# Attention and token-mixing kernel: scores on 64-key halves shifted by 64 queries, value products on row halves in two parts, reciprocal as an operation of its own, a new order

## The chip, the cores and the metric

The kernel runs on one core of one Trainium2 chip. The metric is device time in microseconds (us); the kernel before takes 134.45 us (median of 3 runs, 134.01 to 134.52). TensorE is called PE, its weight loads PEld, VectorE DVE, ScalarE ACT, GpSimd POOL and SyncE SP, as in the profile.

## The reference

The inputs `q`, `k`, `v` have 8 batches, 8 heads, 576 positions and 64 features. A query sees its own key and the 127 before it, with a bias per head that falls with the distance. The attention output, heads side by side, is `x` (8 x 576 x 512), which goes through a token mixer.

```python
scores = scale * np.matmul(q, k.transpose(0, 1, 3, 2))
mask = (rel >= 0) & (rel < window)          # window = 128, rel = query - key
scores = np.where(mask, scores + bias[None], -1000000000.0)
attn = softmax(scores)                      # exp, divided by its sum
attn_out = np.matmul(attn, v)
...
wq = x @ w_q ; wk = x @ w_k                 # 512 -> 64
W_tok = scale * np.einsum('bsd,btd->bst', wq, wk)
mixed = np.einsum('bst,btd->bsd', W_tok, x)
return np.maximum(mixed, 0.0) @ w_out
```

## The kernel before, in words

**Staging.** For each batch `b` the rows of q and k come in as float16 tiles `nat` of 128 positions (operations `Lq`, `Lk`: one DMA for each of four tiles `n`), v as tiles `vt` (`Lv`, with a column of ones beside the 64 values). The last 64 positions of two neighbouring batches come together (`Lt`, `Lv..4`: tiles `natt`, `vtl`). `TQ` and `TT` transpose q and k on PE with an identity, 64 rows of the array at a time, and `ETQ`/`ETT` copy the result to `qkT`.

**Attention.** `QK b,g,u` computes scores of key block `g` (128 keys) for four heads `u`: four products of 64 features by 128 keys by 256 queries, on the upper and lower row half of the array by turns (block 3 has 192 queries and then 64 keys of the tail, so eight products). `EXP` on ACT takes the 1024 columns of a unit to the tile `pt`; `MUL` on DVE multiplies the 2048 columns of both units by `bias`, which also holds the mask. `PV b,t` multiplies `pt` (128 keys by 128 queries as weights) with `vt` (65 columns): 8 heads by 2 key blocks are 16 products, 8 for t = 0, and 32 on column halves for the two tails (t = 4). `X` on DVE takes the reciprocal of the ones column and then multiplies.

**Mixer.** `XT` transposes `x`, `EXT` copies it to `xT`; `WQ`, `WK`, `G` and `MX` are the products of the mixer, `RM` its relu, `OUT` the last product, `EO` copies its result to `osb`, and `DO` writes it to memory, from POOL for batches 0 to 5 and from SP for 6 and 7.

**Order.** Nothing is scheduled at run time. The text `ORDER` lists every operation with its engine and, for PE, its PSUM bank pair (`@PE:2`, or `@PE:01` for one bank; `+3` puts three idle-time products `fill` ahead of it). Each engine runs its own operations in the order of that list. There are 4 bank pairs, 6 tiles `pt`, 4 sets of `nat` and of `vt`. The loads are DMAs that POOL issues one after another; the loop `for d in late: d.deps += issues` makes every output of batches 0 to 5 wait until all loads are issued. `apart` and `lone` (called for every operation) tell the framework which dependences between banks and columns it may drop.

`mode` is the tiling of the array that an operation uses: 0 all of it, 1 row halves (64 x 128), 2 column halves (128 x 64), 3 quarters (64 x 64).

Of the kernel before, what the change touches and what calls it, by code (L numbers as in the profile page):

```python
# [14 lines left out]
P = 128  # L15
# [12 lines left out]
NPT = 6  # L28
HELD = 26
# [12 lines left out]
EXP0.1.0@ACT ones1@DVE QK0.1.1@PE:1+2/30 ETQ0.1.1.1@DVE QK0.0.1@PE:3 Lq1.1@POOL EXP0.1.1@ACT
QK0.2.1@PE:0+1 TT0@PE:2 Lq1.0@POOL EXP0.2.1@ACT ETT0@DVE ETT1@DVE QK0.3.1@PE:1+1 Lv0.0@POOL
MUL0.1@DVE QK0.3.0@PE:2 EXP0.0.1@ACT Lv0.1@POOL EXP0.3.0@ACT MUL0.2@DVE TQ1.2@PE:0+5 Lw0@POOL
Lv0.2@POOL ETQ1.2@ACT MUL0.0@DVE Lv0.3@POOL EXP0.3.1@ACT QK1.3.1@PE:0+6/30 QK1.3.0@PE:2 QK1.2.0@PE:3
Lk2.0@POOL EXP1.3.1@ACT TQ1.0@PE:1 MUL0.3@DVE Lv0.4@POOL ETQ1.0@ACT PV0.0@PE:0 Lq2.0@POOL X0.0@DVE
EXP1.3.0@ACT PV0.1@PE:1 wqq@DVE Lv1.3@POOL QK1.1.1@PE:0 MUL1.3@DVE QK1.1.0@PE:2 EXP1.1.1@ACT
Lq2.1@POOL EXP1.1.0@ACT X0.1@DVE PV0.2@PE:0 Lv1.2@POOL X0.2@DVE EXP1.2.0@ACT Lw1@POOL QK1.0.0@PE:1
QK1.2.1@PE:2 Lk2.1@POOL MUL1.1@DVE EXP1.2.1@ACT PV0.3@PE:0 Lv1.1@POOL XT0.0@PE:3 EXP1.0.0@ACT
MUL1.2@DVE QK1.0.1@PE:2 Lv1.0@POOL EXT0.0@ACT PV0.4@PE:1 X0.3@DVE Lk2.3@POOL EXP1.0.1@ACT  # L50
WQ0.0@PE:30 X0.4@DVE Lq2.2@POOL XT0.1@PE:0 PV1.3@PE:2 EXT0.1@ACT MUL1.0@DVE Lk2.2@POOL XT0.2@PE:31
XT1.2@PE:10 TQ2.0@PE:0 EXT0.2@ACT EXT1.2@ACT Lq2.3@POOL WK0@PE:31 EWQ0.0@DVE ETQ2.0@ACT X1.3@DVE
PV1.2@PE:1 Lk3.2@POOL WQ0.1@PE:30 EWK0@ACT X1.2@DVE PV1.0@PE:0 Lwo0@POOL EWQ0.1@ACT QK2.0.1@PE:2
X1.0@DVE Lwo3@POOL PV1.1@PE:1 EXP2.0.1@ACT Lwo2@POOL QK2.0.0@PE:3 X1.1@DVE G0@PE:00 EXP2.0.0@ACT
Lwo1@POOL XT1.1@PE:2 EG0@DVE Lt2.1@POOL XT1.0@PE:1 EXT1.1@ACT MUL2.0@DVE MX0.0@PE:0 MX0.1@PE:3
EXT1.0@ACT Lv2.0@POOL TQ2.2@PE:2 RM0.0@ACT WQ1.0@PE:10 ETQ2.2@DVE Lt2.0@POOL WQ1.1@PE:11 RM0.1@ACT
WK1@PE:00 Lq3.0@POOL EWQ1.1@DVE QK2.2.0@PE:2 EWQ1.0@DVE EWK1@ACT QK2.2.1@PE:3 Lq3.3@POOL
EXP2.2.0@ACT MX0.4@PE:1 G1@PE:00 RM0.4@DVE Lk3.3@POOL OUT0.3@PE:01 EXP2.2.1@ACT EG1@DVE Lq3.2@POOL
MX1.4@PE:1 QK2.1.1@PE:2 EO0.3@DVE MX1.1@PE:3 RM1.4@ACT EXP2.1.1@ACT Lk3.0@POOL OUT0.1@PE:00
RM1.1@DVE Lq3.1@POOL TT2@PE:1 EO0.1@ACT QK2.1.0@PE:2 MUL2.2@DVE MX1.0@PE:3 EXP2.1.0@ACT Lk3.1@POOL  # L60
OUT1.4@PE:01 ETT2@DVE RM1.0@ACT Lk4.1@POOL OUT0.0@PE:00 ETT3@DVE MUL2.1@DVE Lv2.1@POOL QK2.3.1@PE:2
EO0.0@ACT QK2.3.0@PE:1 TQ3.2@PE:3 EXP2.3.1@ACT EO1.4@DVE Lv2.4@POOL OUT1.1@PE:00 ETQ3.2@DVE
EXP2.3.0@ACT Lv2.3@POOL PV2.0@PE:2 OUT1.2@PE:01 X2.0@DVE Lv3.3@POOL EO1.1@ACT QK3.3.1@PE:3 EO1.2@ACT
MUL2.3@DVE Lv2.2@POOL TQ3.0@PE:1 EXP3.3.1@ACT QK3.3.0@PE:2 OUT1.3@PE:00 Lq4.0@POOL ETQ3.0@DVE
EXP3.3.0@ACT PV2.1@PE:3 Lk4.0@POOL EO1.3@ACT QK3.1.1@PE:1 X2.1@DVE QK3.1.0@PE:2 Lq4.1@POOL
EXP3.1.1@ACT OUT0.2@PE:01 MUL3.3@DVE Lv3.1@POOL EXP3.1.0@ACT XT2.0@PE:3 QK3.0.1@PE:1 Lq4.2@POOL
EXT2.0@DVE OUT1.0@PE:00 EXP3.0.1@ACT MUL3.1@DVE Lk4.3@POOL PV2.2@PE:2 EO0.2@ACT QK3.2.0@PE:3
Lq4.3@POOL EO1.0@ACT X2.2@DVE PV2.3@PE:1 EXP3.2.0@ACT QK3.2.1@PE:0 Lv3.2@POOL X2.3@DVE PV2.4@PE:2
EXP3.2.1@ACT TQ4.0@PE:3 Lk4.2@POOL X2.4@DVE XT2.1@PE:1 ETQ4.0@ACT WQ2.0@PE:00 Lk5.2@POOL EXT2.1@DVE
XT2.2@PE:01 QK3.0.0@PE:2 EWQ2.0@DVE XT3.2@PE:10 Lv3.0@POOL EXT2.2@ACT QK4.0.0@PE:3 MUL3.2@DVE  # L70
EXP3.0.0@ACT WK2@PE:11 Lt4.1@POOL WQ2.1@PE:00 EXP4.0.0@ACT EWK2@DVE QK4.0.1@PE:2 MUL3.0@DVE
Lk5.3@POOL G2@PE:01 EWQ2.1@ACT EXP4.0.1@ACT Lq5.3@POOL PV3.2@PE:3 EG2@DVE MX2.1@PE:0 X3.2@DVE
EXT3.2@ACT Lq5.2@POOL MX2.0@PE:2 RM2.1@ACT TQ4.2@PE:1 RM2.0@DVE Lq6.3@POOL PV3.3@PE:3 ETQ4.2@ACT
OUT2.3@PE:00 Lt4.0@POOL X3.3@DVE PV3.0@PE:2 EO2.3@ACT QK4.2.0@PE:1 Lv4.1@POOL X3.0@DVE PV3.1@PE:3
EXP4.2.0@ACT Lv4.0@POOL QK4.2.1@PE:0 X3.1@DVE OUT2.0@PE:20 EXP4.2.1@ACT Lq5.1@POOL MUL4.0@DVE
XT3.0@PE:1 EO2.0@ACT QK4.1.1@PE:3 Lk5.1@POOL XT3.1@PE:0 EXT3.0@ACT OUT2.2@PE:21 EXT3.1@DVE
EXP4.1.1@ACT Lq5.0@POOL MUL4.2@DVE QK4.1.0@PE:1 TT4@PE:0 EO2.2@ACT Lk5.0@POOL TQ5.2@PE:3
EXP4.1.0@ACT ETT4@DVE WQ3.1@PE:20 ETQ5.2@DVE Lv4.2@POOL WK3@PE:21 ETT5@ACT EWQ3.1@ACT Lk6.1@POOL
QK4.3.1@PE:1 MUL4.1@DVE EWK3@ACT QK4.3.0@PE:0 MX2.4@PE:3 EXP4.3.1@ACT G3@PE:20 Lv4.3@POOL RM2.4@DVE
WQ3.0@PE:21 EXP4.3.0@ACT Lq6.0@POOL EG3@DVE PV4.0@PE:1 EWQ3.0@DVE MX3.1@PE:3 X4.0@DVE PV4.1@PE:2  # L80
Lq6.2@POOL RM3.1@ACT MX3.0@PE:0 X4.1@DVE TQ5.0@PE:1 Lq6.1@POOL RM3.0@ACT QK5.3.1@PE:3 ETQ5.0@DVE
OUT2.1@PE:20 Lv4.4@POOL EXP5.3.1@ACT Lv5.3@POOL QK5.3.0@PE:0 EO2.1@DVE XT4.0@PE:1 EXP5.3.0@ACT
QK5.0.0@PE:3 EXT4.0@DVE OUT3.1@PE:21 Lk6.0@POOL MUL4.3@DVE EXP5.0.0@ACT Lk6.2@POOL QK5.2.0@PE:1
QK5.0.1@PE:0 WQ4.0@PE:20 EO3.1@ACT MUL5.3@DVE Lk6.3@POOL PV4.2@PE:3 EXP5.0.1@ACT OUT3.3@PE:21
Lv5.0@POOL X4.2@DVE EXP5.2.0@ACT PV4.3@PE:0 Lv5.1@POOL MUL5.0@DVE QK5.1.1@PE:3 EWQ4.0@ACT MX3.4@PE:1
EO3.3@ACT Lk7.3@POOL OUT3.2@PE:20 EXP5.1.1@ACT RM3.4@DVE X4.3@DVE Lk7.2@POOL PV4.4@PE:1 EO3.2@ACT
QK5.2.1@PE:3 X4.4@DVE Lt6.1@POOL TQ6.0@PE:0 EXP5.2.1@ACT TQ6.2@PE:2 ETQ6.0@DVE Lt6.0@POOL
OUT3.0@PE:10 ETQ6.2@ACT Lq7.2@POOL MUL5.2@DVE QK5.1.0@PE:3 EO3.0@ACT XT4.2@PE:11 Lv5.2@POOL
XT4.1@PE:0 QK6.1.1@PE:2 EXP5.1.0@ACT EXT4.1@DVE OUT3.4@PE:10 Lq7.3@POOL EXT4.2@DVE EXP6.1.1@ACT
MUL5.1@DVE WK4@PE:11 Lq7.0@POOL PV5.0@PE:0 EO3.4@ACT QK6.1.0@PE:3 X5.0@DVE Lk7.1@POOL EWK4@ACT  # L90
# [76 lines left out]
def kernel(  # L167
# [51 lines left out]
    def two(bank):  # L219
        return pairs[bank[0]]  # L220

    held = []

    def hold(i):
        held.append(i.ins)

    def mm(*a, **k):
        hold(nc.tensor.matmul(*a, **k))  # L228

    def tp(*a):  # L230
        hold(nc.tensor.transpose(*a))  # L231

# [658 lines left out]
```

## Time and profile before

| | |
|---|---|
| median of 3 runs | 134.45 us (134.01 to 134.52) |
| profiled execution, span of its instructions | 132.4 us |
| PE | 121.7 us busy, 2349 products |
| ACT | 112.9 us busy |
| DVE | 112.3 us busy |
| POOL | 109.6 us busy (almost all DMA issue) |
| PE from 28.00 to 127.40 us | 98.80 us busy of 99.40 |

The profile is one execution. Its span runs from the first to the last instruction and is 2.05 us shorter than the median of the runs, which also hold what lies around the span. An operation's length on PE is read here from its first product's start to the next operation's first start, since matmuls are pipelined and the shown ends overlap. The names of the program stand for lines: all products are on L228, transposes on L231, loads on L383, outputs on L797 and L800, `EXP` on L556, `MUL` on L566, reciprocal and multiplication on L613 and L614.

### The profile page before, as it was taken

The page shows a single profiled execution, that of the slowest core. Times are in us where ns is not written, and L with a number is a line of the kernel's source. Part 1 is how long each engine was busy: PE and PEld are TensorE (multiplying, and loading weights), DVE is VectorE, ACT ScalarE, POOL GpSimd, SP SyncE. Part 2 cuts the span into 40 slices and gives each one's busy share as a digit, 9 for nine tenths or more (in the row PEclk, how much of TensorE's full clock was granted, in tenths as well). Part 3 has the DMA queues.
Part 4 walks back from the last instruction along what each step waited for, and adds up shares of the span by engine and source line. Part 5 has one row for each costly group of instructions (what it writes and reads, how often), then busy time and mean ns, then how long its engine had stood idle before and what let it go on. Part 6 is the DMA issues. An engine that isn't in the chain of part 4 may idle for free.

```text
span 132.4 us, 5423 instructions
## 1 busy us (share of the span) xinstructions
PE 121.7 (92%) x2349; PEld 77.6 (59%) x2349; DVE 112.3 (85%) x206; ACT 112.9 (85%) x163; POOL 109.6 (83%) x147
## 2 busy tenths in 40 slices
PE   6988795888999999999999999999999999999970
PEld 2343364676774565767677667567567656863430
DVE  6776958997978999999999999999999999982530
ACT  5999779986999999999999999999999897554730
POOL 7999879999999999999999999999968509790000
PEclk9999999999999999999999999999999999999998
DMA  3999999999999999999999999999999936999775
GB/s 119 275 148 155 157 158 152 149 151 149 189 156 158 156 155 153 157 153 154 156 154 156 153 152 153 156 157 152 157 212 376 374 125 228 334 303 367 285 211 185
DMA packets 110663, 25.12 MB, mean 190 GB/s; under 512 B 104816, under 2 KB 107888, under 8 KB 110640
## 3 DMA queue, kind: packets, MB, share of 16 engines
q0 software_dynamic: 108128, 21.37, 178.4%
q1 hardware_dynamic: 2512, 3.41, 7.5%
q8 instruction: 18, 0.29, 0.8%
q14 instruction: 5, 0.04, 0.1%
HBM read 29.62 MB, written 9.44 MB: 295 GB/s over the span
## 4 chain that ended last, share of the span: by engine, by line
PE 77%; ACT 7%; POOL 6%; DMA 6%; issue 1%; POOLq 0%; ACTq 0%
PE pair L228 67%; PE pair L231 10%; DMA nat<-in_q_dram 6%; ACT pt L556 5%; POOL nat L383 4%; ACT qkT L241 1%; POOL natt L383 1%; ACT osb L235 1%; POOL ident masks.py:199 0%; POOL ident masks.py:197 0%; POOL xT L339 0%; POOL xT L340 0%; POOL wint L311 0%; ACTq L556 0%; POOLq L311 0%
## 5 line engine op out<-in xcount | busy, mean ns | idle before, releaser
L556 ACT ACTIVATE pt<-pair 128x1024 f16<-128x1024 f32 x64 | 63.2, 1033 | 1.6 <-PE pair L228 1.3
L383 POOL DMA_DIRECT2D vt<-in_v_dram x32 | 31.7, 1138 | 0.9 <-DMA nat<-in_q_dram 0.9
L228 PE MATMUL pair<-wout_sb,rm 128*128 128x512 f16 (+1 forms) x132 | 32.4, 374 | 0.0
L383 POOL DMA_DIRECT2D nat<-in_k_dram x29 | 29.2, 1059 | 0.5 <-DVE pt L566 0.5
L383 POOL DMA_DIRECT2D nat<-in_q_dram x29 | 29.0, 1058 | 0.1
L566 DVE TENSOR_TENSOR pt<-pt,bias 128x2048 f16<-128x2048 f16 x24 | 29.0, 1217 | 0.0
L228 PE MATMUL pair<-vt,pt 128*128 128x65 f16 (+1 forms) x512 | 21.4, 194 | 2.9 <-ACT pt L556 1.6
L228 PE MATMUL pair<-qkT 64*128 64x256 f16 (+2 forms) x320 | 23.3, 250 | 0.8 <-DVE qkT L243 0.3
L228 PEld LDWEIGHTS <-pt 128*128 128x128 f16 (+1 forms) x576 | 19.0, 100 | 8.1 <-issue 6.0
L614 DVE TENSOR_TENSOR x<-pair,inv 128x512 f16<-128x512 f32 x32 | 22.1, 692 | 1.1
L235 ACT COPY osb<-pair 128x512 f32<-128x512 f32 (+1 forms) x29 | 16.7, 585 | 4.3 <-PE pair L228 4.0
L797 POOL DMA_DIRECT2D out_dram<-osb x24 | 13.5, 604 | 6.4 <-ACT osb L235 4.7
L228 PEld LDWEIGHTS <-rm 128*128 128x128 f16 x132 | 10.9, 97 | 11.9 <-issue 1.9
L228 PEld LDWEIGHTS <-qkT 64*128 64x128 f16 x320 | 10.8, 94 | 8.3 <-issue 4.7
L731 ACT ACTIVATE rm<-pair 128x1024 f16<-128x1024 f32 (+1 forms) x12 | 11.3, 956 | 1.4 <-PE pair L228 1.2
L228 PE MATMUL pair<-fill 128*128 128x512 f16 x33 | 10.6, 453 | 1.7 <-DVE fill L364 1.2
L243 DVE COPY qkT<-pair 128x2048 f16<-128x2048 f16 (+1 forms) x12 | 10.4, 884 | 1.5 <-PE pair L231 1.5
L231 PEld LDWEIGHTS <-nat 64*128 64x128 f16 x512 | 9.1, 95 | 4.0 <-ACT nat L235 1.3
L231 PE MATMUL pair<-identh,nat 64*128 64x64 f16 x512 | 10.4, 190 | 1.1 <-DMA nat<-in_q_dram 0.7
L566 DVE TENSOR_TENSOR pt<-pt,biasl 128x2048 f16<-128x2048 f16 x8 | 9.7, 1219 | 1.6 <-ACT pt L556 1.6
L228 PE MATMUL pair<-xT,wqq_sb 128*128 128x256 f16 (+1 forms) x64 | 10.4, 287 | 0.0
L241 ACT COPY qkT<-pair 128x1024 f32<-128x1024 f32 (+1 forms) x10 | 8.2, 834 | 1.5 <-PE pair L231 1.4
(66 smaller groups left out, 161.8 us busy)
## 6 DMA issues: line engine op xcount, KB each, us to landing
out_dram<-osb POOLq DMA_DIRECT2D x24, 256.0 KB, 4.7
vt<-in_v_dram POOLq DMA_DIRECT2D x32, 128.0 KB, 6.0
nat<-in_q_dram POOLq DMA_DIRECT2D x28, 128.0 KB, 5.7
nat<-in_k_dram POOLq DMA_DIRECT2D x28, 128.0 KB, 5.8
out_dram<-osb SPq DMA_DIRECT2D x7, 256.0 KB, 2.6
out_dram<-osb POOLq DMA_DIRECT2D x6, 128.0 KB, 4.3
nat<-in_k_dram SPq DMA_DIRECT2D x1, 512.0 KB, 3.8
nat<-in_q_dram SPq DMA_DIRECT2D x1, 512.0 KB, 4.7
```

The lines of the kernel that those rows point to most:

```text
L228: hold(nc.tensor.matmul(*a, **k))
L231: hold(nc.tensor.transpose(*a))
L235: hold(nc.scalar.copy(out_ap, in_ap))
L241: hold(nc.scalar.copy(out_ap.bitcast(FP32), in_ap.bitcast(FP32)))
L243: hold(nc.vector.tensor_copy(out=out_ap, in_=in_ap))
L383: op = add(kind, b, part, (eng,), deps, lambda o: q.dma_start(out=dst, in_=src), size=size)
L556: nc.scalar.activation(out=pt[:, u, 0:1024], in_=two(s.bank).rearrange("p e c -> p (e c)"), func=AF.Exp, scale=SCALE)
L566: nc.vector.tensor_tensor(out=pt[:, :, 0:1024], in0=pt[:, :, 0:1024], in1=bt, op=ALU.mult)
L614: nc.vector.tensor_tensor(out=x.rearrange("p (g h d) -> p g h d", g=2, h=4), in0=pxv[:, :, :, 0:64], in1=inv.unsqueeze(3).broadcast_to([P, ...
L731: hold(nc.scalar.activation(out=out_ap, in_=in_ap, func=AF.Relu, scale=WSCALE))
L797: q.dma_start(out=out[b, P * st:P * st + P, c], in_=osb)
```

## The change

**Scores.** A unit now has two halves of 64 keys. The lower half takes 192 queries from its own first key on, the upper half (keys 64 to 127) takes 192 queries that start 64 later. Both have the same 192 columns of distances, so `bias`, `EXP` and `MUL` are 192 columns wide where they were 256: 768 columns for `EXP`, 1536 for `MUL`. Each unit is eight products of 64 x 64 (twelve for block 3) on quarters of the array.

**Value products.** In `pt` a head now has a slot of 256 columns, 192 of data and 64 of zeros in front of it (`gaps`, six operations at the start). Each half of 64 keys is read with its own shift, the zeros standing for queries outside. So a `PV` becomes products of 64 rows on the row halves of the array. The two row halves may not add to the same bank at once; so `PV` does heads 0 to 3 on one row half and 4 to 7 on the other, and a second part `PW` does the same with the row halves exchanged. Between the two, SP carries a mark: `T` is an empty instruction on SP that waits for `PV`, and `PW` waits for it.

**The rest.** `R` (reciprocal) and `X` (multiplication) are two operations. The zeroing of `qkT` and of half of `vtl` and the 16 small ones-writes are gone; one write of ones and the six `gaps` take their place. The rule that outputs wait for all load issues is gone. `ORDER` is new throughout.

```diff
-zeros@DVE iota@POOL Lf1.0@SP pads@POOL dist@DVE mask@DVE Lf0.0@SP ident@POOL ones2@DVE bias0@ACT
+iota@POOL Lf0.0@SP ones@DVE gaps0@ACT gaps3@ACT ident@POOL Lf1.0@SP dist@DVE mask@DVE Lh1.1@POOL
...
-    pt_s = [cpool.tile([P, 2, 1024], F16, name=f"pt{i}") for i in range(NPT)]
+    pt_s = [cpool.tile([P, 9 * HW], F16, name=f"pt{i}") for i in range(NPT)]
...
+    def behind(i, op):
+
+        for j in op.insts[-2:]:
+            tc.add_manual_dep(i, j.name, mybir.DependencyInfo(
+                mybir.DependencyClass.Sync, mybir.DependencyReason.DATA), reason="other half, same bank")
...
+    def mk_gaps(i):
         def em(o):
-            for t in vt_s[i]:
-                nc.vector.memset(t[:, :, D:D + 1], 1.0)
...
+            cpw(o.eng, pt_s[i].rearrange("p (s c) -> p s c", c=HW)[:, :, 0:64],
+                zero.rearrange("p (s c) -> p s c", c=64))
...
-    def segs(g):
-        return [(g, P * g, 256, 0)] if g < 3 else [(3, 384, 192, 0), (4, 512, 64, 192)]
+    def segs(g, c):
+
+        k0 = P * g + 64 * c
+        if g == 3 and c:
+            return [(k0, k0, 128, 0), (512, 512, 64, 128)]
+        return [(k0, k0, KW, 0)]
+
+    def data(t, lo, n):
+
+        return t[:, 64:64 + 8 * HW].rearrange("p (s c) -> p s c", c=HW)[:, lo:lo + n, 0:KW]
...
-                for kb, q0, wd, c0 in segs(g):
-                    for e in range(2):
-                        r = slice(64 * e, 64 * e + 64)
-                        mm(ps[:, e, 256 * a + c0:256 * a + c0 + wd],
-                                         t[r, 1, hp, P * kb:P * kb + P],
-                                         t[r, 0, hp, q0:q0 + wd], start=True, stop=True)
+                for e, c in ((0, 0), (1, 1), (0, 1), (1, 0)):
+                    r = slice(64 * e, 64 * e + 64)
+                    for k0, q0, n, at in segs(g, c):
+                        mm(ps[64 * c:64 * c + 64, e, KW * a + at:KW * a + at + n],
+                           t[r, 1, hp, k0:k0 + 64], t[r, 0, hp, q0:q0 + n], start=True, stop=True)
...
-            nc.vector.tensor_tensor(out=pt[:, :, 0:1024], in0=pt[:, :, 0:1024], in1=bt, op=ALU.mult)
+            nc.vector.tensor_tensor(out=data(pt, 0, 8), in0=data(pt, 0, 8), in1=bt, op=ALU.mult)
...
+        def em(swap):
+            def go(o):
+                px = two(o.bank or o.same.bank)
+                kbs = [(qt, 0)] + ([(qt - 1, 128)] if qt else [])
+                for i in range(4):
+                    for n, (kb, c) in enumerate(kbs):
+                        for u in range(2):
+                            r = u ^ swap
+                            h, at, cols = spot(i, u)
+                            at += c + 64 * (1 - r)
+                            k = slice(64 * r, 64 * r + 64)
+                            mm(px[:, u, cols], pt_s[turn(b, kb) % NPT][k, at:at + P],
+                               vt_s[b % NV][kb][k, h, 0:65], start=(swap + i + n == 0),
+                               stop=(swap == 1 and i == 3 and n == len(kbs) - 1))
+                if swap:
+                    behind(held[0], o.deps[0])
+
+            return go
...
+        p = add("PV", b, qt, PE, need, em(0), banks=2, mode=mode, size=size)
+
+        def mark(o):
+            hold(nc.sync.nop())
+            behind(held[0], p)
+
+        t = add("T", b, qt, SP, [p], mark)
+        w = add("PW", b, qt, PE, [t, p], em(1), mode=mode, size=size)
...
-    for d in late:
-        d.deps += issues
```

The first place is on PE: a score unit of block 3 followed by a value product, before (a unit of block 2 there) and now. The columns are line, instruction, output and inputs; 64 x or 128 x is the output's partitions and columns.

```order
L228 LDWEIGHTS qkT0_87
L228 MATMUL pair1_136<-qkT0_87 128x256
L228 LDWEIGHTS pt1_108
L228 MATMUL pair3_138<-vt30_101,pt1_108 128x65 [waits DVE_49]
L228 LDWEIGHTS pt2_109
L228 MATMUL pair3_138<-vt31_102,pt2_109 128x65
```

```order
L240 LDWEIGHTS qkT1_88
L240 MATMUL pair2_121<-qkT1_88 64x128
L240 LDWEIGHTS qkT1_88
L240 MATMUL pair2_121<-qkT1_88 64x64
L240 LDWEIGHTS qkT1_88
L240 MATMUL pair2_121<-qkT1_88 64x192
L240 LDWEIGHTS pt4_95 [waits SP_sequencer_49]
L240 MATMUL pair1_120<-vt_89,pt4_95 128x65
```

The score products are narrower and more, and the first weight load of a second part `PW` waits for SP where a value product waited for DVE alone.

The second place is on POOL: the end of the loads. Before, the last k load of batch 7 (`nat_84`), then v loads (`vt`), and outputs (`osb`) only behind the last of them; each waits for one of the eight semaphores `DMASW0` to `DMASW7`, that is for the landing of the DMA eight issues earlier.

```order
L383 DMA nat_83<-in_q_dram 128x8x64 [waits DMASW2_49]
L383 DMA nat_84<-in_k_dram 128x8x64 [waits DMASW3_49]
L383 DMA vt_97<-in_v_dram 128x8x64 [waits DMASW4_49]
L383 DMA vt_102<-in_v_dram 128x8x64 [waits DMASW5_49,PE_49]
L383 DMA vt_104<-in_v_dram 128x8x64 [waits DMASW6_49]
```

```order
L394 DMA nat30_83<-in_q_dram 128x8x64 [waits DMASW1_49]
L394 DMA natt1_86<-in_q_dram 64x16x64 [waits DMASW2_49]
L394 DMA vt_89<-in_v_dram 128x8x64 [waits DMASW3_49]
L856 DMA out_0_dram<-osb512_1291 128x512 [waits DMASW4_49,DVE_49]
L394 DMA vt_89<-in_v_dram 128x8x64 [waits DMASW5_49]
L856 DMA out_0_dram<-osb512_1531 128x512 [waits DMASW6_49,DVE_49]
L394 DMA vt_89<-in_v_dram 128x8x64 [waits DMASW7_49,PE_49]
L856 DMA out_0_dram<-osb512_1189 128x512 [waits DMASW0_49]
```

Behind the last q load of batch 7, outputs now stand between the v loads of batches 6 and 7; they come from batches 0 to 5, finished long before.

More of the change, by code (lines that the diff above doesn't have):

```diff
@@ L42 @@
[L42 to L47, printed above, removed]
@@ L119 @@
+EO7.3.1@ACT OUT7.1@PE:30 RM7.0@DVE DO7.3.0@SP DO7.3.1@SP OUT6.0@PE:31 EO7.1@DVE OUT6.1@PE:20 EO6.0@ACT
+DO6.0@SP OUT7.2@PE:21 EO6.1@ACT DO7.1@SP RM7.4@ACT OUT7.0@PE:20 EO7.2@ACT DO6.1@SP DO7.2@SP OUT7.4@PE:21
+EO7.0@DVE DO7.0@SP EO7.4@ACT DO7.4@SP
 """
```

317 lines of the change are left out of this document (167 added, 150 removed).

## The prediction

> **What bounds the kernel now.** I read the page's busy times, then the chain that ended last, then busy time in four stretches, to see which engine sets the end and where.
>
> ```profile
> span 132.4 us, 5423 instructions
> PE 121.7 (92%) x2349; PEld 77.6 (59%) x2349; DVE 112.3 (85%) x206; ACT 112.9 (85%) x163; POOL 109.6 (83%) x147
> PE 77%; ACT 7%; POOL 6%; DMA 6%; issue 1%; POOLq 0%; ACTq 0%
> ...
> 9.14 7.34 DMA nat<-in_q_dram
> 22.11 4.70 ACT pt L556 x5
> 115.84 11.51 PE pair L228 x102
> ...
> 0.00:17.00 17.00, 13.66 (x179) 6.32 (x179) 13.08 (x43) 14.17 (x23) 15.40 (x26) 1.00 1.64 170
> 17.00:28.00 11.00, 8.40 (x199) 6.12 (x190) 8.98 (x16) 10.57 (x12) 10.47 (x13) 1.00 2.27 152
> 28.00:127.40 99.40, 98.80 (x1980) 64.67 (x1980) 90.19 (x149) 86.95 (x127) 83.69 (x110) 1.00 1.92 195
> 127.40:132.40 5.00, 0.81 (x8) 0.48 (x5) 0.00 (x0) 1.21 (x3) 0.00 (x0) 0.92 0.65 227
> ```
>
> The last four rows give the stretch, its length, then the busy time of PE, PEld, DVE, ACT, POOL, the granted clock, DMA share and GB/s. Until 17 us the kernel waits for loads; from 17 to 28 us ACT is the busiest (10.57 of 11.00: the scores' exponentials); from 28 us to the chain's last product at 115.84 + 11.51 = 127.35 us PE is busy for 98.80 of 99.40 us at full clock; 5.0 us of copies and outputs end the span. So nothing that DVE or ACT save after 28 us is worth anything by itself. What PE saves counts, unless PE then has to wait. What could it wait for? POOL, that issues the loads:
>
> ```profile
> 84.81 1.33 POOL L383 DMA_DIRECT2D nat<-in_k_dram  x1
> 85.67 1.28 POOL L383 DMA_DIRECT2D vtl<-in_v_dram  x1
> 86.48 1.34 POOL L383 DMA_DIRECT2D nat<-in_q_dram  x1
> 87.35 1.35 POOL L383 DMA_DIRECT2D nat<-in_k_dram  x1
> 88.22 7.48 POOL L383 DMA_DIRECT2D vt<-in_v_dram  x8
> 95.15 2.20 POOL L797 DMA_DIRECT2D out_dram<-osb  x3
> 98.02 0.55 POOL L797 DMA_DIRECT2D out_dram<-osb  x1 [0.67 <-DMA vt<-in_v_dram]
> ...
> nat<-in_k_dram POOLq DMA_DIRECT2D x28, 128.0 KB, 5.8
> vt<-in_v_dram POOLq DMA_DIRECT2D x32, 128.0 KB, 6.0
> ...
> 97.23 0.64 PE L231 MATMUL pair<-identh,nat 64*128 64x64 f16 x32
> ```
>
> A load occupies POOL for 0.87 us (eight v loads start over 95.15 - 88.22 = 6.93 us), whatever PE does, and lands 5.8 to 6.0 us after its issue. The k load at 87.35 us is the last q or k load of the program; it lands at 93.2 us and its transposes start at 97.23 us. That is a slack of only 4 us, at a place from which PE still runs 127.35 - 97.23 = 30.1 us. The load stream is thus a second bound close under the first.
>
> **The price of PE work.** The timeline of PE gives an operation's length as the distance of starts.
>
> ```profile
> 42.59 1.04 PE L228 MATMUL pair<-wout_sb,rmt 128*128 128x512 f16 x4
> 43.47 1.03 PE L228 MATMUL pair<-wout_sb,rm 128*128 128x512 f16 x4
> 44.43 0.62 PE L228 MATMUL pair<-qkT 64*128 64x192 f16 x16
> ...
> 86.51 0.39 PE L228 MATMUL pair<-qkT 64*128 64x256 f16 x4
> 86.83 0.66 PE L228 MATMUL pair<-vt,pt 128*128 128x65 f16 x16
> 87.43 0.39 PE L228 MATMUL pair<-qkT 64*128 64x256 f16 x4
> 87.75 0.63 PE L228 MATMUL pair<-x,wkn 128*64 128x256 f16 x8
> 88.21 0.28 PE L228 MATMUL pair<-xtl,wkn 128*64 128x256 f16 x2
> 88.42 0.41 PE L231 MATMUL pair<-identh,natt 64*128 64x64 f16 x16
> 88.66 0.38 PE L228 MATMUL pair<-qkT 64*128 64x256 f16 x4
> ...
> 112.83 1.13 PE L228 MATMUL pair<-vt,pt 128*128 128x65 f16 x32
> 113.80 0.60 PE L228 MATMUL pair<-xT,wqq_sb 128*128 128x256 f16 x4
> ...
> 26.85:27.47 0.62, 0.62 (x32) 1.00 2.31 144
> ```
>
> Two value products on the whole array take 113.80 - 112.83 = 0.97, so 0.485 each, when the next operation uses the array in the same way; 0.60 (86.83 to 87.43) when it goes on to row halves. The last product takes 0.88 (42.59 to 43.47) and then 0.96 (to 44.43) in the same comparison. A change of tiling thus costs about 0.10 us. A score unit, 0.32 with a change behind it, is 0.22: two pairs of 256 columns.
>
> *Scores.* Eight products of 192 columns. If four run at once, a unit is two rounds of 192 columns at the rate of the pairs, 0.22 x 192/256 = 0.167 us. If only two run at once, it is four rounds, 0.33. Both sides have rows: sixteen transposes on row halves take 0.24 (88.42 to 88.66), and ten products of 256 columns on column halves 0.67 - 0.10 (87.75 to 88.42), 0.114 a pair, so both ways of halving overlap fully; the two together no row shows. Weights must come in fast enough too: the 32 tail products, a 64-column load each, took 0.62 - 0.10 (the last row, from their first start to the next operation's), 0.016 a load; eight would take 0.13, less than 0.167. I take 0.167: 64 units save 64 x 0.055 = 3.5 us.
>
> The Trainium skill (TensorEngine Tiling (Array Packing), Restrictions) says that column tiling disables fast weight load, and its page TensorE: Matmul & The Clock Gate (LDWEIGHTS) gives columns / 1.2 ns for a load, 53 ns for 64 columns. Eight such loads in a row would make a unit 0.43 us, an estimate from that page; the 0.016 us a load of the row above speaks against it.
>
> *Value products.* Sixteen products on the whole array become twice sixteen on row halves, that run in pairs; the sixteen transposes of 0.24 are the same shape, 64 columns for 65. So 2 x 0.24 = 0.48 for 0.485. The bound above is a part that pays as much as one on the whole array, 0.97. Taken: nothing. The parts now share their tiling with the transposes, but the scores no longer do: counted along the order of PE, changes of tiling go from 115 to 122 (without `fill`), +0.7 us.
>
> *The wait of the second part.* A `PW` can start when `PV` has drained, SP has seen it and PE has seen SP. Nearest rows:
>
> ```profile
> 110.10 0.42 PE L228 MATMUL pair<-vt,pt 128*128 128x65 f16 x8
> ...
> 110.63 0.21 DVE L613 RECIPROCAL inv<-pair 128x8 f32<-128x8 f32 x1 [0.17 <-PE pair L228]
> ```
>
> The products of 110.10 end at 110.52 and DVE starts 0.11 later. From the start of the last product: 0.19 of drain, 0.11 to SP, as much back, 0.4 us. PE is in order, so the whole rest of its queue stands behind a waiting `PW`. In the new order every `PV` behind the first two batches but four has 0.33 us or more of other work in front of its `PW` (a score unit and two changes of tiling, say, 0.37). With 0.4 us that leaves 2.3 us of stalls over all 36, 1.3 of it before 28 us, 1.0 behind, of that 0.1 in batches 6 and 7. With 0.3 us it is 1.3.
>
> *ACT and DVE.*
>
> ```profile
> L556 ACT ACTIVATE pt<-pair 128x1024 f16<-128x1024 f32 x64 | 63.2, 1033 | 1.6 <-PE pair L228 1.3
> L566 DVE TENSOR_TENSOR pt<-pt,bias 128x2048 f16<-128x2048 f16 x24 | 29.0, 1217 | 0.0
> ```
>
> With 768 for 1024 columns the exponential falls to between 0.775 and 1.03, I take 0.82; the multiplication from 1.22 to between 0.91 and 1.22, I take 0.95. Over 64 and 32 of them that frees 13.6 and 8.6 us on engines with no part in the bound; PE covers it. Only before 28 us it shows, where the sixteen exponentials gain some 3 us but three `gaps` and more copies of `qkT` are put on ACT, and the first `PW` stall. Taken: 1 us, bounds 0 and 2. `R` apart from `X`, fewer small writes and the new zeros lie beside the first loads: nothing.
>
> **The sum.** PE alone would end at 127.35 - 3.5 + 0.7 - 1.0 (start) + 1.0 (stalls after 28 us) - 0.6 (the idle time of that stretch now) = 123.95, say 124.0. But loads do not move. In the new order the last q load of batch 7 is POOL's 98th transfer where the last one was its 100th: 87.35 - 2 x 0.87 = 85.6, or up to 1 us sooner if POOL loses less at the start; I take 85.1, and with 5.8 it lands at 90.9. PE by its own work would be there at 124.0 less the 34.6 us that follow, 89.4. So its transposes wait. From there the new order leaves PE more to do than before: three last products (3 x 0.87), two `MX` and a `WQ` (0.2, 0.2, 0.45), a `TT` (0.24), eleven score units at 0.167 for seven at 0.22 (0.3) and five changes (0.5), 4.5 us in all; 30.1 + 4.5 = 34.6. PE ends at 90.9 + 34.6 = 125.5, the span at 130.5: 1.9 us under 132.4. The median lies 134.45 - 132.4 = 2.05 above the span: 132.6 us, 1.4% faster. By its own work PE would save 3.4 us; 1.5 of them go into waiting for the load stream.
>
> **Rivals.** (a) *Quarters don't overlap* (the change doesn't do what it says): a unit at 0.33 costs 64 x 0.11 = 7.0 more than before, PE's own path decides: 124.0 + 3.5 + 7.0 = 134.5, the span 139.5 and the time 141.6; at 0.22, with weights as the limit, 134.6. No row shows four at once; both halvings do overlap. It decides from 0.19 us a unit. By the skill's 53 ns a load in series, as above, it would be still slower. 0.12.
>
> (b) *The round trip over SP is long*: at 1.0 us instead of 0.4 the stalls in batches 6 and 7 grow to 4.7 us, and all of them lie behind the last q load: 132.6 + 4.6 = 137.2, slower. It decides from 0.7 us. For: no row shows SP between two PE instructions. Against: DVE's 0.11. 0.12.
>
> (c) *Outputs between the loads delay the last v.* Fourteen outputs now precede the last v load; with a place in the eight-deep ring free only when the transfer eight before has landed (the 0.67 us wait at 98.02), it goes out at 102 to 105 and lands at 108 to 111, where PE wants it at about 108.5. Up to 2.5 us: 132.6 to 135.1, say 134. 0.14.
>
> (d) *The loads do not bind*, because they land early enough or the way from the last q load is shorter than counted: PE's own path, 124.0 + 5.0 + 2.05 = 131.05, or 130.05 where the start gains the upper bound; 130.5. Against it stands POOL's unvarying 0.87. 0.12.
>
> **How the numbers follow.** My forecast has 0.50; its own range is 131.4 to 134. To hold 8 in 10 I reach down to 130.4, most of (d), and up to 137.2, which takes (c), (b) and the light half of (a), and leaves out the heavy one. Within 0.5%, about what a measurement here can tell from no change, is 133.8 to 135.1. Faster: 0.46 of the forecast, (d) 0.12, 0.04 of (c), 0.02 of (b): 0.64. Same: 0.04, 0.05 of (c), 0.03 of (b), 0.02 of (a): 0.14. Slower: 0.05, 0.07 and 0.10: 0.22.
>
> **What would show it.** Score units alone at 0.17 from start to start, 0.27 with a change of tiling; the two value parts at 0.24 each; a `PW` no more than 0.4 us behind its `PV`; the exponential near 820 ns and the multiplication near 950; DVE and ACT each about 10 to 14 us less busy; POOL still full to 85 us; the last q transposes starting when their load lands, near 91 us, with idle PE in front of them; PE ending near 125.5. I am wrong if these transposes start without a wait, if a unit takes over 0.2 us, if PE waits for SP in batches 6 and 7, or if PE stalls for v behind 100 us.

## The result and the profile after

The changed kernel takes 150.44 us (median of four runs, 148.43 to 152.89) against 134.37 us for the kernel before on the same chip, 16.1 us more, where 132.6 us were forecast and 137.2 was the upper end of the range. Two of the four, 151.35 us and the profiled 152.89 us, count as slow, so the ratio on record, 1.1107 with a 95% interval of 1.1048 to 1.1166, is that of the two fast ones, 149.54 and 148.43 us: 149.0 in the mean, 14.6 us over before. The experiments are set against these 149.0 us; the busy times, stalls and clock of the kernel after are those of the profiled execution.

The page of the kernel after, cut to the rows that answer to those of before (the clock row gives the granted clock of TensorE in tenths, in 40 slices; the `q8` row gives packets, MB and share of the instruction queue):

```profile
span 150.8 us, 6984 instructions
PE 129.4 (86%) x3120; PEld 83.2 (55%) x3120; DVE 100.5 (67%) x178; ACT 103.5 (69%) x175; POOL 110.6 (73%) x148
PEclk9999999959999999699599999999959999999999
q8 instruction: 24, 0.39, 1.0%
PE 73%; ACT 12%; issue 9%; DVE 3%; SPq 0%; ACTq 0%
L574 ACT ACTIVATE pt<-pair 128x768 f16<-128x768 f32 x64 | 48.5, 819 | 10.7 <-PE pair L240 10.3
L240 PE MATMUL pair<-vt,pt 64*128 64x65 f16 (+1 forms) x1024 | 26.8, 197 | 4.9 <-issue 4.4
L586 DVE TENSOR_TENSOR pt<-pt,bias 128x1536 f16<-128x1536 f16 x24 | 22.3, 951 | 2.3 <-ACT pt L574 2.2
```

The same two rows in the page of the kernel before:

```profile
PEclk9999999999999999999999999999999999999998
q8 instruction: 18, 0.29, 0.8%
```

ACT and DVE did get lighter, as intended: 112.9 to 103.5 us and 112.3 to 100.5. But ACT now waits 10.3 us for PE's scores, PE is busy 86% of the span where it was 92%, and "issue" has grown from 1% to 9% of the chain that ended last: time in which PE waits for nothing that the profile can name. The clock row has four slices well under full speed, at 5 or 6 tenths; the kernel before has 9 in all but the last.

The view of waits of the kernel after (engine and line, what it waited for, us in total, times, longest) shows where PE stood:

```profile
PE pair L240 <- issue: 7.9, 5, 2.1
PE pair L243 <- issue: 3.1, 3, 1.8
PE pair L240 <- ACT pt L574: 1.6, 4, 0.9
...
PEld L240 <- SPq L651: 0.7, 3, 0.2
```

Eight waits without a releaser, one of them of only 0.4 us (at 23.64 us), sum to 11.0 us. The waits for SP's mark, which one rival was built on, sum to 0.7 us. The timeline of PE (start, length, operation, and in brackets the idle time ahead and what ended it) at five of those places, each with the row ahead of it:

```profile
58.57 0.20 PE L240 MATMUL pair<-vtl,pt 64*64 64x65 f16 x2
60.37 0.24 PE L240 MATMUL pair<-vt,pt 64*64 64x65 f16 x5 [1.61 <-issue]
...
68.16 0.41 PE L240 MATMUL pair<-vt,pt 64*128 64x65 f16 x16
70.72 0.63 PE L240 MATMUL pair<-x,wkn 128*64 128x256 f16 x8 [2.15 <-issue]
...
91.61 0.20 PE L240 MATMUL pair<-vt,pt 64*64 64x65 f16 x2
93.20 0.22 PE L240 MATMUL pair<-vtl,pt 64*64 64x65 f16 x2 [1.39 <-issue]
...
101.88 0.23 PE L240 MATMUL pair<-vt,pt 64*128 64x65 f16 x4
103.40 0.57 PE L240 MATMUL pair<-vt,pt 64*128 64x65 f16 x26 [1.30 <-issue]
...
105.81 0.86 PE L243 MATMUL pair<-identh,nat 64*128 64x64 f16 x48
108.50 0.38 PE L243 MATMUL pair<-identh,nat 64*128 64x64 f16 x14 [1.82 <-issue]
```

Four of the five break off in the middle of an operation, among products of one kind, and the profile names no operand that they waited for. Counting PE's instructions up to each long stall (a weight load and a product make two) gives the pattern. The starts of the 16,384-byte packets on the instruction queue, read from the trace, stand beside it:

```
kernel after: distance of starts over 0.8 us behind 20 us
last start   distance   instructions so far    modulo 256   packet starts
 26.81 us     1.66 us      958                   190           26.20 us
 36.95        1.07        1468                   188           35.69
 58.57        1.80        2490                   186           57.93
 68.38        2.34        3000                   184           68.33
 91.62        1.58        4024                   184           90.86
101.91        1.49        4536                   184          100.97
106.49        2.02        4792                   184          106.21
```

All seven come a whole number of 256 instructions apart, to within a few (the rest of a division by 256 is 184 to 190), whatever the operation. 16,384 bytes over 256 instructions are 64 bytes each; the kernel before has 2 x 2349 = 4698 such instructions and 18 packets, the kernel after 2 x 3120 = 6240 and 24. Each stall begins up to 1.3 us behind the start of a packet, and all seven end 2.27 to 2.44 us behind it. This fits a PE that had run to the end of the code it held and stood until the next piece, the next packet, was there; experiment 5 tests it. That is the theory below (F); the rivals were that the stall belongs to an operation, or that the array work or waits of the new order carry the loss.

A stall also costs behind itself. Busy time in stretches around the first two stalls of that list behind 50 us (PE, PEld, DVE, ACT, POOL, then the granted clock, DMA share and GB/s):

```profile
56.00:58.50 2.50, 2.35 (x105) 1.86 (x107) 2.12 (x5) 2.46 (x5) 2.50 (x4) 1.00 2.42 159
58.50:60.40 1.90, 0.29 (x17) 0.18 (x10) 0.79 (x1) 1.90 (x3) 1.90 (x3) 1.00 2.43 152
60.40:62.00 1.60, 1.60 (x29) 0.70 (x31) 1.13 (x3) 0.05 (x2) 1.60 (x3) 0.81 2.43 155
62.00:64.00 2.00, 2.00 (x80) 2.00 (x78) 1.50 (x2) 1.09 (x2) 2.00 (x4) 0.50 2.40 158
64.00:66.00 2.00, 2.00 (x45) 1.52 (x40) 0.90 (x2) 1.12 (x3) 2.00 (x4) 0.80 2.46 154
66.00:68.40 2.40, 2.40 (x124) 2.15 (x120) 2.00 (x5) 1.50 (x5) 2.40 (x5) 1.00 2.44 161
68.40:70.70 2.30, 0.17 (x12) 0.15 (x5) 1.10 (x3) 0.98 (x1) 2.30 (x4) 1.00 2.39 151
70.70:72.00 1.30, 1.28 (x37) 1.08 (x38) 0.00 (x0) 0.51 (x2) 1.30 (x3) 0.86 2.43 155
72.00:74.00 2.00, 2.00 (x28) 1.28 (x23) 1.21 (x2) 1.64 (x3) 2.00 (x4) 0.50 2.39 159
```

About 1 us behind each of these two stalls the granted clock falls to 0.50 for 3.4 us (by the mean clocks of the three rows from 60.40 us: 0.6, 2.0 and 0.8 us of it), while PE is busy again. Not every stall is followed by it: behind those at 91.62 and 101.91 us the clock stays at 1.00. Over the span, (1 - 0.952) x 150.8 = 7.2 us of full clock are missing; before it was (1 - 0.997) x 132.4 = 0.4. The executions of 149.54 and 148.43 us had a mean clock of 0.988 and 0.972, 1.8 and 4.1 us missing.

### The profile page after: what moved, and what is told of

Read it like the earlier page. It is cut to its first block, busy times and chain, and to the rows that moved or that the text cites. A ratio compares the mean times of both kernels' runs of the same rounds, so it can differ in the third digit from the quotient of the medians.

```text
span 150.8 us, 6984 instructions
## 1 busy us (share of the span) xinstructions
PE 129.4 (86%) x3120; PEld 83.2 (55%) x3120; DVE 100.5 (67%) x178; ACT 103.5 (69%) x175; POOL 110.6 (73%) x148
## 4 chain that ended last, share of the span: by engine, by line
PE 73%; ACT 12%; issue 9%; DVE 3%; SPq 0%; ACTq 0%
PE pair L240 62%; PE pair L243 11%; ACT pt L574 8%; ACT qkT L259 1%; ACT xT L259 1%; ACT osb L247 1%; DVE x L671 1%; DVE nat L261 0%; DVE xtl L671 0%; DVE qkT L249 0%; DVE inv L668 0%; ACT wkn L247 0%; DVE zero L375 0%; ACT rmt L790 0%; SPq L651 0%
## 5 line engine op out<-in xcount | busy, mean ns | idle before, releaser
L574 ACT ACTIVATE pt<-pair 128x768 f16<-128x768 f32 x64 | 48.5, 819 | 10.7 <-PE pair L240 10.3
L240 PE MATMUL pair<-vt,pt 64*128 64x65 f16 (+1 forms) x1024 | 26.8, 197 | 4.9 <-issue 4.4
L240 PEld LDWEIGHTS <-pt 64*128 64x128 f16 (+1 forms) x1088 | 21.5, 100 | 13.3 <-issue 7.7
L586 DVE TENSOR_TENSOR pt<-pt,bias 128x1536 f16<-128x1536 f16 x24 | 22.3, 951 | 2.3 <-ACT pt L574 2.2
L240 PE MATMUL pair<-qkT 64*64 64x192 f16 (+2 forms) x576 | 20.3, 243 | 2.4 <-ACT pt L574 1.1
L240 PEld LDWEIGHTS <-qkT 64*64 64x64 f16 x576 | 11.7, 106 | 9.5 <-issue 5.0
L792 DVE TENSOR_SCALAR rm<-pair 128x1024 f16<-128x1024 f32 (+1 forms) x13 | 14.1, 1094 | 2.6 <-PE pair L240 2.4
L668 DVE RECIPROCAL inv<-pair 128x8 f32<-128x8 f32 x36 | 6.8, 200 | 11.8 <-PE pair L240 11.6
L259 ACT COPY xT<-pair 128x512 f32<-128x512 f32 (+2 forms) x19 | 8.6, 465 | 6.6 <-PE pair L243 6.3
L240 PE MATMUL pair<-zero 128*128 128x512 f16 x36 | 11.7, 472 | 1.6 <-DVE zero L375 1.2
L249 DVE COPY osb<-pair 128x512 f32<-128x512 f32 x15 | 10.2, 683 | 3.9 <-PE pair L240 3.9
```

The lines of the kernel that those rows point to most:

```text
L240: return hold(nc.tensor.matmul(*a, **k))
L249: hold(nc.vector.tensor_copy(out=out_ap, in_=in_ap))
L259: hold(nc.scalar.copy(out_ap.bitcast(FP32), in_ap.bitcast(FP32)))
L574: nc.scalar.activation(out=data(pt, 4 * u, 4).rearrange("p (e a) c -> p e a c", e=2), in_=two(s.bank)[:, :, 0:2 * KW].rearrange("p e (a c) ...
L586: nc.vector.tensor_tensor(out=data(pt, 0, 8), in0=data(pt, 0, 8), in1=bt, op=ALU.mult)
L668: nc.vector.reciprocal(out=box["inv"], in_=px(64))
```

## The experiments

**1. Fewer value products.** In the kernel after, the products with the key block before are left out.

```diff
-                kbs = [(qt, 0)] + ([(qt - 1, 128)] if qt else [])
+                kbs = [(qt, 0)]
```

> The changed kernel with the value products of the key block before left out of PV and PW (tiles 1 to 3 of each batch, 384 products and 384 weight loads fewer; the output is then not the reference's). Theory F (PE's code comes in pieces of 16 KB, 256 instructions, at best one per about 4.9 us while the loads run, and PE stands still at a piece's edge when it ran ahead): 3 pieces less, 15 us, so 134 to 138 us, and long stalls at fewer places. Rival W (PE lost the time in the row-half products themselves): 48 parts lose 0.12 us each, 5.8 us, so 143 us.

Measured: 139.36 us (139.03 to 139.68), 1.039 of before [1.030, 1.048]; 21 pieces, three long stalls of 4.9 us together behind 20 us (at 188 and 180 over a multiple of 256), clock 0.961. The saving of 9.6 us (from 149.0) ends nearer to F's bounds than to W's, but misses both, and the edit takes array work away too. It says that this work is dear, not why.

**2. More instructions in the kernel before.** Each value product is cut into 33 and 32 columns.

```diff
+                for lo, hi in ((0, 33), (33, 65)):
...
-                        mm(px[:, h // 4, 65 * (h % 4):65 * (h % 4) + 65],
-                           pt_s[turn(b, kb) % NPT][:, u, c:c + P], vt_s[b % NV][kb][:, h, 0:65],
...
+                        mm(px[:, h // 4, 65 * (h % 4) + lo:65 * (h % 4) + hi],
+                           pt_s[turn(b, kb) % NPT][:, u, c:c + P], vt_s[b % NV][kb][:, h, lo:hi],
...
```

> The kernel before, with each value product cut into two products of 33 and 32 columns: same numbers, same tiling, no second part, no SP, but 448 products and 448 weight loads more (896 PE instructions, 3.5 pieces of 256). Theory F: stalls of 1 to 2 us without a cause in the trace appear at edges of 256 instructions, 138 to 143 us. Rivals (the second part's wait over SP, the row halves, the quarters): none of them is in it, PE's work grows by 28 x 0.03, so 135 to 136 us.

Measured: 145.58 us, 1.0855 [1.0746, 1.0963]. Above both expectations, and inconclusive. The timeline of PE in this kernel shows why:

```profile
56.98 0.98 PE L228 MATMUL pair<-vt,pt 128*128 128x33 f16 x32
57.89 0.39 PE L228 MATMUL pair<-qkT 64*128 64x256 f16 x4
```

32 products with whole-array weights take 57.89 - 56.98 = 0.91 us with the change of tiling behind them, 0.81 without: 25 ns for each at 33 columns, where the uncut ones took 30 ns at 65. Cutting therefore added 0.81 - 0.485 = 0.33 us of array time to each of the 24 operations that have a block before, 7.8 us of the 11, where it was to be nearly free. The long stalls of this kernel sum to 2.9 us, of which 1.2 lie at no edge of 256.

**3. Fewer loads in the kernel after, and in the kernel before.** The loads of q, k, v and tails of batches 4 to 7 are left out of both.

```diff
-        op = add(kind, b, part, (eng,), deps, lambda o: q.dma_start(out=dst, in_=src), size=size)
+        gone = kind in ("Lq", "Lk", "Lv", "Lt") and b >= 4
+        op = add(kind, b, part, (eng,), deps, (lambda o: None) if gone else (lambda o: q.dma_start(out=dst, in_=src)),
+                 size=size)
```

> The changed kernel without the loads of q, k, v and tails of batches 4 to 7 (they compute on the tiles of batches 0 to 3, so the output is not the reference's). PE has every instruction that it had. Theory F with the loads' descriptors as the reason for the slow code: behind about 55 us pieces come at 3.5 us, the long stalls there go, 136 to 141 us. F without the loads as the reason: stalls stay at the same instructions, 147 to 149 us. Rival L (PE waits for loads, as predicted): the time falls too, but the stalls without a cause remain.

> The kernel before without the loads of q, k, v and tails for batches 4 to 7: the control for the same edit of the kernel after, which saved 7 to 9 us. Theory F: before has 18.4 pieces and only 2.7 us of excess over usual durations, so it gains little from free DMA engines, 130 to 134. Rival L (loads hold up the work in both kernels alike, by data that comes late): it gains as much as the kernel after did, 125 to 128.

Measured: after 143.37 us (5.6 less than 149.0), before 134.42 us against 134.4, ratio 0.9994 [0.9955, 1.0033], 0.4 us above the range that F gave. The control excludes that the loads hold up both kernels alike: before gains nothing. In the kernel after the packets of code, never less than 4.84 us apart from 28 to 100 us, now come down to 3.46 us; the stalls at 2490, 4536 and 4792 instructions go under 0.8 us, those at 3000 and 4024 shrink to 0.95, and the stalls ahead of 50 us, where loads still run, stay (1.95 and 2.17 us). Timing each packet from the moment at which PE passes the edge one piece earlier (edges taken 184 to 190 over a multiple of 256) shows why. In the kernel after it starts a median of 2.45 us behind that moment (15 packets from 28 us to the landing of the last load, 1.3 to 3.2 us); here, behind 55 us, a median of 1.05 us (16 packets, up to 2.4 us, two of them even ahead). So the loads' traffic delays the code, and delayed code is what costs. F's number (136 to 141) was too hopeful: the early stalls remained.

**4. Quarters alone.** In the kernel before, scores go to quarters of the array, 256 queries each.

```diff
-                    for e in range(2):
+                    for e, c in ((0, 0), (1, 1), (0, 1), (1, 0)):
                         r = slice(64 * e, 64 * e + 64)
-                        mm(ps[:, e, 256 * a + c0:256 * a + c0 + wd],
-                                         t[r, 1, hp, P * kb:P * kb + P],
+                        mm(ps[64 * c:64 * c + 64, e, 256 * a + c0:256 * a + c0 + wd],
+                                         t[r, 1, hp, P * kb + 64 * c:P * kb + 64 * c + 64],
```

> The kernel before with its scores alone on quarters of the array: each product of 64 x 128 x 256 becomes two of 64 x 64 x 256, 320 products and 320 weight loads more (2.5 pieces), the same columns in flight. If quarters overlap four ways a unit stays at 0.22 us. Theory F: 135 to 139 us, stalls at edges of 256 instructions. Rival Q (quarters or changes to them are slow): every unit longer than 0.25 us, 138 us and more, without long stalls.

Measured: 139.54 us, 1.0404 [1.0251, 1.0556], clock 1.000, one stall of 1.1 us. A unit takes 0.242 us against 0.229 with half as many products: four quarters do run at once. The 5.2 us go mostly into tiling: the scores no longer share it with the transposes around them, 44 more changes (159 against 115, without `fill`) at 0.10 us, 4.4 us, and 64 x 0.013 = 0.8 us for the units. The stall is the one that the kernel before has too, at no edge of 256. Time and stalls are thus as rival Q said, though a unit stays under its 0.25 us, and 0.5 us above F's range. With 5338 instructions the kernel is not short of code: more instructions alone are not enough.

**5. The same work, other places in the code.** The 22 products of 512 columns that fill PE's time ahead of the first transposes are cut into 88 of 128.

```diff
-        for _ in range(op.fills):
-            mm(one(op.spare), fill[:, 0:P], fill, start=True, stop=True)
+        k = 4 if op.name == "TQ0.0.0" else 1
+        for n in range(k * op.fills):
+            w = 512 // k
+            mm(one(op.spare)[:, 0:w], fill[:, 0:P], fill[:, 0:w], start=True, stop=True)
```

> The kernel after, with the 22 products of 512 columns that keep TensorE busy ahead of its first transposes cut into 88 of 128 columns: the same work for the array, but every later instruction of TensorE stands 132 instructions further on. Theory F (code pieces of 256 instructions come too late): the long stalls after 25 us lie at the same instruction counts as before, 182 to 188 over a multiple of 256, and so before other products; time 147 to 153. Rival O (a stall belongs to an operation: its bank, its operands or its wait): the stalls stay before the same products, and their counts are 132 higher, 58 to 64 over a multiple of 256; time the same.

Measured: 155.12 us (154.29 to 155.94), a little above the range. The stalls, in the same count as above:

```
instructions so far   kernel after              with the code shifted by 132
   958                inside tail products      inside transposes of x
  1468                inside transposes of x    (under 0.8 us)
  2490                inside tail products      inside value products
  2746                (under 0.8 us)            inside transposes of q, k
  3000                behind value products     inside value products
  3256                (under 0.8 us)            inside scores
  4024                inside tail products      inside value products
  4280                (under 0.8 us)            inside transposes of x
  4536                inside value products     (under 0.8 us)
  4792                inside transposes of q, k behind scores
  5048                (under 0.8 us)            inside transposes of tails
```

The timeline of PE in this kernel, at 2490, 3000 and 4024:

```profile
58.34 0.37 PE L240 MATMUL pair<-vt,pt 64*128 64x65 f16 x11
59.49 0.26 PE L240 MATMUL pair<-vt,pt 64*128 64x65 f16 x5 [0.78 <-issue]
...
67.93 0.27 PE L240 MATMUL pair<-vt,pt 64*128 64x65 f16 x6
69.28 0.45 PE L240 MATMUL pair<-vt,pt 64*128 64x65 f16 x18 [1.09 <-issue]
...
88.90 1.02 PE L240 MATMUL pair<-vt,pt 64*128 64x65 f16 x46
91.56 0.45 PE L240 MATMUL pair<-vt,pt 64*128 64x65 f16 x18 [1.65 <-issue]
```

All nine stalls sit 184 to 190 over a multiple of 256, none of them 58 to 64 over one. In the kernel after, the stalls at 2490 and 4024 split the tail products (`vtl`); here, at the same counts, they split plain value products. The place in the code decides and not the operation: rival O is refuted.

**6. Whole rows again.** In the kernel after, each pair of half-row value products becomes one of 128 rows; the tail products stay.

```diff
...
                         for u in range(2):
-                            r = u ^ swap
+                            if swap:
+                                pass
+                                continue
                             h, at, cols = spot(i, u)
-                            at += c + 64 * (1 - r)
-                            k = slice(64 * r, 64 * r + 64)
-                            mm(px[:, u, cols], pt_s[turn(b, kb) % NPT][k, at:at + P],
-                               vt_s[b % NV][kb][k, h, 0:65], start=(swap + i + n == 0),
+                            mm(px[:, u, cols], pt_s[turn(b, kb) % NPT][:, at + c + 64:at + c + 64 + P],
+                               vt_s[b % NV][kb][:, h, 0:65], start=(i + n == 0),
...
```

> The kernel after with each pair of half-row value products made one product of all 128 rows again and the second part left empty (SP's mark and the order stay). It reads the columns of the first half's place for both halves and uses flatter distance weights, so the attention's values are not the reference's; the score units, exponentials, multiplies and all later work are as in the kernel after. TensorE has 5346 instructions against 6242, 20.9 pieces of 256 against 24.4, and the same array time by the trace (0.485 us for 16 products of 128 rows, 0.48 for 32 on row halves). Theory F: without the 512 added products the stalls shrink, and the time comes to what the prediction summed without code fetch, 131 to 138, at most three stalls over 1 us. Rival S (the quartered scores, the tilings or the new order carry the loss): 145 or more.

Measured: 141.16 us (140.68 to 142.05), 1.0511 [1.0435, 1.0586]. Of the 14.6 us, 7.8 are gone with 448 products (the expectation says 512) that, by the trace, cost the array nothing extra: 0.496 us for 32 on row halves, 0.48 to 0.50 for 16 of whole rows. Three long stalls are left (4.5 us), again at 184 to 190 over a multiple of 256. The last of them, 2.1 us, is not code alone: the profile has PE wait there for a multiplication on DVE, which ends at 101.05 us, 0.17 us before PE goes on, while the packet of 98.28 us would have let it go on near 100.6. Behind one of the three the clock still halves, as a stretch of this kernel shows:

```profile
76.00:88.00 12.00, 10.15 (x238) 6.63 (x237) 7.51 (x15) 8.64 (x14) 12.00 (x15) 0.86 2.44 154
```

The time lies 3 us over F's range and 4 under S's; experiment 7 asks what is left.

**7. Whole rows and fewer loads.** Edits 3 and 6 together.

> Both edits at once: value products on all 128 rows (20.9 pieces of code) and no loads of q, k, v and tails for batches 4 to 7. So far the kernel after took 150.4 us, with fewer loads 143.4, with full rows 141.2; the kernel before 134.4 with and without those loads. Theory F: with pieces less than 4.3 us apart behind 55 us and fewer of them wanted, no stall over 1 us is left behind 55 us, and the time is 132 to 137, near what the prediction summed. Rival W (what full rows leave over the sum, 8.6 us, is time of the array, tilings or waits between engines in the new order, not fetched code): 139 to 142, as with full rows alone.

Measured: 137.77 us (137.28 to 138.2), 1.0265 [1.0232, 1.0298], 0.8 us over F's range. The page and the waits of PE in this kernel:

```profile
PEclk9999999999999999999999999999999999999999
q8 instruction: 21, 0.34, 1.0%
...
PE pair L240 <- ACT pt L576: 2.7, 8, 0.9
PE pair L240 <- DVE zero L375: 1.2, 1, 1.2
PE pair L243 <- DMA nat<-in_k_dram: 1.1, 3, 0.5
```

No stall over 0.8 us is left behind 20 us, no product waits on "issue", and the clock holds (0.999). Of the 14.6 us, 11.2 are gone (149.0 - 137.8), against 0 for the same lighter load stream in the kernel before. The 3.4 us that remain are not code: the view shows waits for exponentials and for the early k loads instead, and a unit's array time is longer than was summed.

The runs side by side (instructions: weight loads and products of PE; pieces: packets of code; stalls: number and sum of the distances of starts over 0.8 us behind 20 us; clock lost: one minus the mean granted clock, by the span; stalls and clock are of the profiled execution, which for the kernel after took 152.89 us):

```
kernel                          instructions  pieces  stalls       clock lost   time us
before                          4698          18      1,  1.1 us   0.4 us       134.4
before, fewer loads             4698          18      1,  1.1      1.1          134.4
before, quarters                5338          21      1,  1.1      0.0          139.5
before, products cut            5594          22      3,  2.9      2.0          145.6
after                           6240          24      7, 12.0      7.2          149.0
after, code shifted             6372          25      9, 15.6      9.2          155.1
after, fewer loads              6240          24      6,  7.7      3.7          143.4
after, no block before          5472          21      3,  4.9      5.4          139.4
after, whole rows               5344          21      3,  4.5      2.1          141.2
after, whole rows, fewer loads  5344          21      0,  0.0      0.1          137.8
```

Of these 34 stalls 29 lie 180 to 190 over a multiple of 256. The other five do not: the one of each of the first three rows, one of `before, products cut` and one of `after, fewer loads`.

## Why the prediction was wrong

**The step that failed** is the first line of its sum: "PE alone would end at 127.35 - 3.5 + 0.7 - 1.0 (start) + 1.0 (stalls after 28 us) - 0.6 (the idle time of that stretch now) = 123.95". It takes PE's time as array time plus waits for other engines, and lets the number of instructions cost nothing as long as products overlap (the value products, doubled in number, are "Taken: nothing"). The change raises it from 4698 to 6240. If each kind of operation is given the lower quartile of its own lengths, PE's work behind 28 us is about 97 us before and 98 after, so nearly equal; but it holds 3968 instructions before, 24.4 ns each, and 5282 after, 18.6 ns each. While the loads ran a packet started some 2.45 us after PE had passed the edge before, and PE could go on 2.3 us behind its start: 4.75 us for 256 instructions, 18.6 ns each, an estimate from these two figures. It is no fixed floor, since in experiment 1, with all loads, some packets came 4.2 us apart. Before, code came faster than the array used it; after, the array ran into it wherever small products lie together: two value parts pass 64 instructions in 0.48 us, 7.5 ns each. PE's last product ended near 146 us, not 125.5. No rival had this mechanism, and the page's row of the instruction queue, which bears on it, has no part in the prediction.

**What was right.** A value part alone takes 0.24 to 0.255 us (0.24 said), a change of tiling 0.10, an exponential 819 ns (820), a multiplication 951 (950); DVE and ACT are 11.8 and 9.4 us less busy (10 to 14 said, so ACT falls just short).

**What was mis-sized.** A score unit alone takes 0.19 us (median) and not 0.167, with a change of tiling 0.292; 64 x 0.023 = 1.5 us more than the sum had. Rival (a) was to decide from 0.19: the unit stands on that edge and still saves 0.04 us over before. The Trainium skill (TensorEngine Tiling (Array Packing), Restrictions) has column tiling disable fast weight load; the prediction's estimate of 0.43 us a unit adds to that eight loads one after another. Eight loads and eight products in 0.19 us exclude that estimate; no run here shows whether each load was a slow one that ran beside others.

**The second part's wait on SP.** 2.3 us were taken; 0.7 us in three waits were measured, all ahead of 25 us and none in batches 6 and 7. Rival (b) is refuted.

**The load stream.** The forecast let the last q transposes wait for their load until near 91 us. In the kernel after, POOL issues that load 1.6 us later than said, and PE reaches the 64 transposes of batch 7 (32 need this load, from 106.25 us on) long behind it, as the timelines of POOL and of PE show:

```profile
86.75 1.06 POOL L394 DMA_DIRECT2D nat<-in_q_dram  x1
...
105.78 0.89 PE L243 MATMUL pair<-identh,nat 64*128 64x64 f16 x50
```

With 5.6 us from issue to landing the load is there at 92.4 us, some 14 us early. The first of the prediction's signs of being wrong, transposes that start without a wait, came true. In the kernel of experiment 7, without long stalls, PE reaches the same transposes at 93.09 us, not at the 89.4 of the sum; so the forecast wait would hardly have come up without the late code either, though that kernel has fewer loads. The load stream binds nothing by late data here; it acts through the code that it delays. Rivals (c) and (d) were not put to the test that they describe. The last v load did go out late, at 105.22 us, as (c) said, but PE was late by then too: its one wait at a v load, 0.4 us at 87.35 us, lies ahead of the first outputs. And that the loads do not bind, as (d) said, came about because PE was late, not because they landed early: 92.4 us against 90.9 said.

**What the sum misses without the code.** Whole rows with fewer loads come to 137.8 us, 5.2 over the forecast; PE's last product ends 2.6 us later than before, where the sum's 124.0 has it 3.35 earlier. The units explain 1.5 of these 6 us. Lengths over the lower quartile behind 28 us add up to 7.5 to 8 us there and to 2.7 before, about 5 more: the new order leaves PE short waits, for ACT and the early k loads among others, that the forecast put at nothing behind cover. Which rows of the order make them was not tried one by one.

**The split of the 14.6 us.** Shown: 11.2 us go with fewer products and lighter loads, together with every code stall and the lost clock, while the lighter loads alone do nothing for the kernel before. Argued, not shown apart: that within it the stalls themselves (12.0 us from start to start in the profiled execution) and the clock behind them (7.2 us there, 1.8 and 4.1 in the executions of 149.54 and 148.43 us) make up the sum; they overlap with waits that would have stood there anyway. Open: what holds a packet for some 2.45 us while loads run. The fetches that ended a stall started at most 0.4 of a piece before PE stood for want of it, the others 0.4 to 1.0 before: no fetch started more than about one piece ahead. None of these kernels beats the kernel before.

## What to carry to other kernels

Cutting a product into pieces that overlap cost the array nothing here, but it did cost code: count an engine's instructions over the stretch that binds, and put nanoseconds per instruction beside what the instruction queue brings while the loads run. Long waits with no releaser, in the middle of like products and a fixed number of instructions apart, were code that had not come; where you meet them, shift the code by a known number of instructions, and see whether they stay at the count or at the operation. Where two edits each seem to explain a loss, run both alone, both together, and the second one on the kernel before.

## What the runs showed of the hardware

Code comes to PE in packets of 16,384 bytes, one for every 256 of its instructions: 18 packets for 4698, 24 for 6240. From 28 to 100 us, while the loads ran, they were at least 4.84 us apart in the kernel after, with few loads down to 3.39 us, and PE went on 2.27 to 2.44 us behind the start of the packet it stood for. A packet started a median of 2.45 us after PE had passed the edge one piece earlier while the loads ran, and of 1.05 us behind 55 us with the loads of batches 4 to 7 left out. The Trainium skill (Runtime: NRT & Kernel Launch, Instruction fetch mechanics) gives blocks of 16 KiB and 256 instructions too, which the trace bears out; it also says that crossing a block is mostly hidden, since instructions issue slower than they are fetched. Here they issued faster in places, 7.5 ns each, and it cost several per cent; the measurement decides.

The granted clock fell to 0.50 behind idle gaps of 1.61 and 2.15 us, after PE was busy again, and stayed at 1.00 behind gaps of 1.39 and 1.30 us in the same trace. The length of the gap alone does not decide: with whole rows (experiment 6) it fell behind a gap of 1.34 us and not behind one of 1.83. The Trainium skill (TensorE: Matmul & The Clock Gate, Why this matters for your kernels) warns of idle gaps over some 3 us; in this trace it fell behind shorter ones.

A product with a weight load for the whole array took 25 ns at 33 columns, and 0.485 / 16 = 30 ns at 65; on row halves, in pairs, 0.496 / 32 = 15.5 ns each at 65. Four quarters ran at once: eight products of 192 columns in 0.19 us.
